# Casting GpSimd loads of q and k in a windowed-attention and spectral-mixing kernel

## The chip, the cores and the metric

The kernel runs on one core of a Trainium2 chip. The core has a matrix engine (PE, with its weight loads shown apart as PEld), a vector engine (DVE), an activation engine (ACT), GpSimd (POOL), a queue engine that only issues transfers (SP), and 16 DMA engines that serve all queues. The metric is the device time of one execution in microseconds. Before the change it is 444.54 us, the median of three runs (444.14 to 446.43).

## The reference, cut to what matters

Attention with a window of 128 positions and a linear distance bias runs over batch 8, 8 heads, 576 positions and 64 features. Its output is mixed over positions in the spectrum: the first 64 modes are each multiplied by a complex 512 x 512 matrix of their own, and the result goes back through the inverse transform. All tensors are float32 in memory.

```python
scores = scale * q @ k.T + slope[h] * -(i - j)       # kept where 0 <= i - j < 128
x = softmax(scores) @ v                              # (8, 576, 512) over all heads
X = rfft(x, axis=1)[:, :64]
Yr = einsum(Xr, w_r) - einsum(Xi, w_i)               # w_r, w_i: (64, 512, 512)
Yi = einsum(Xr, w_i) + einsum(Xi, w_r)
u = x + irfft(Yr + 1j * Yi, n=576)
out = u + relu(u @ w_ch)
```

The 128 matrices of w_r and w_i are 1 MB each and 127 of them are read; q, k and v are 9.4 MB each.

## The kernel before, in words

**Attention.** One unit is a batch and four of its heads: 16 units. For each unit the kernel loads q, k and v, casts them to bf16 on DVE (`cast`), transposes q and k on PE in nine blocks into one PSUM tile (`transpose`, L250), copies that to SBUF as `qkT` (`evacuate`, mostly on ACT, L256), forms the scores (`score`, L271 and L284), applies exp on ACT (`exp`, L294), the mask on DVE (`mask`, L305), multiplies by v (`value`, L331) and divides by the sums on DVE (`norm`, L346 and L347). After the second unit of a batch, `spectrum` and `channels` turn the batch's output into its first 64 modes, `XC`.

**The order of work.** Each engine executes its instructions in the order in which they are written here. `STAGE` lists the steps of one stage with their lags: a step with lag 1 works in stage s on unit s - 1, one with lag -2 on unit s + 2. A stage takes steps of several units, so that all engines have work. There are some preparatory steps before stage 0, written out in the main function.

**The loads.** `load` issues the transfers of q, k and v on SP. The fp32 buffers `raw` hold two units of each. A load of unit u + 2 is issued at the end of the cast of unit u, in whose buffer it lands. One q or k load is 576 KB: 128 partitions, two rows of 2304 bytes each. A v load is five transfers in rows of 512 bytes.

**Early weights.** While attention runs, weights are already read as bf16 by casting loads that POOL issues (`load_w`, L459), into 14 buffers of the pool `early` (one before the stages, one at the end of each of stages 1 to 13) and then into seven stretches of `raw` that are no longer needed (`LATER`, two after stage 13, two after stage 14, three after stage 15). The weight of a stage stands behind a one-element copy on POOL, the gate (L533), which waits for that stage's first `norm`.

**After attention.** The weights go through PE in the order of the modes (L838), four products each. SP loads them plain into a pool of 6 buffers (`NWA`, fp32 read as bf16 by taking every second half-word), later 2 more (`NWB`); eight of the early buffers are used a second time by casting loads on POOL (`AGAIN`). Beside this the finished modes are transposed, and products with w_ch and inverse transforms are made. After the last weight the remaining modes are added and the output is written.

**POOL at the start.** In its order: the identity, the integer tables, the distance tables (`distances`, L147 to L168), the constant parts of the v buffers (`fixtures`, L136 to L140, for two buffers), the first early weight between the two, the end of the Fourier table (L102 to L104), and a memset of `XC` (L496).

Of the kernel before, what the change touches and what calls it, by code (L numbers as in the profile page):

```python
# [10 lines left out]
FP32 = mybir.dt.float32  # L11
BF16 = mybir.dt.bfloat16
# [21 lines left out]

NC = 24


STAGE = (
    ("exp", 1, 0), ("score", 0, 0), ("exp", 0, 0), ("value", 0, 1), ("spectrum", None, 2),
    ("cast", "v", 0), ("score", 2, 0), ("channels", None, 2), ("transpose", "k", -1),  # L40
    ("cast", "k", -2), ("exp", 2, 0), ("norm", 0, 1), ("cast", "q", -3), ("score", 3, 0),
    ("mask", 1, 0), ("value", 1, 1), ("evacuate", "k", -1), ("mask", 0, 0), ("exp", 3, 0),
    ("transpose", "q", -2), ("evacuate", "q", -2), ("score", 1, -1), ("norm", 1, 1),
)
# [62 lines left out]
class _Attention:  # L107


    def __init__(self, tc, ctx, q, k, v, consts, x, XC, raw):  # L110
        self.tc, self.nc = tc, tc.nc
        self.q, self.k, self.v = q, k, v
        self.ident, self.F, self.FT = consts
        self.x, self.XC = x, XC
        B, H, S, _ = q.shape
        self.S, self.NG = S, H // 4
        self.units = [(b, g) for b in range(B) for g in range(self.NG)]
        self.raw = raw
        self.mid = ctx.enter_context(tc.tile_pool(name="amid", bufs=2))
        self.ps = ctx.enter_context(tc.tile_pool(name="aps", bufs=1, space=PSUM))  # L120
        fix = ctx.enter_context(tc.tile_pool(name="afix", bufs=1))
        self.table = fix.tile([P, H, 2, 2 * P], BF16, name="mask")
        self.bias = fix.tile([P, H, 2, 2 * P], BF16, name="bias")
        self.vb = [fix.tile([P, 2, 4, 2, 2 * W], BF16, name=f"vb{i}") for i in range(2)]
        self.vt = [fix.tile([P, 4, 2, W], BF16, name=f"vt{i}") for i in range(2)]
        self.qkT = [fix.tile([P, 2, 2, (FULL + 1) * P], BF16, name=f"qkT{i}") for i in range(2)]
        self.att = [fix.tile([P, FULL * 8 * P + 64], BF16, name=f"att{i}") for i in range(2)]
        self.loaded, self.casted, self.open = {}, {}, {}

    def fixtures(self, i):  # L130
        nc = self.nc
# [66 lines left out]
    def load(self, w, u):  # L198
        nc = self.nc
        if u >= len(self.units):  # L200
            return
        b, g = self.units[u]
        hs = slice(4 * g, 4 * g + 4)
        if w == "v":
            t = self.raw[w][:, u % 2]
            sv = self.v[b, hs]
            for h in range(4):
                nc.sync.dma_start(
                    out=t[:, :2, h],
                    in_=sv[h, : FULL * P].rearrange("(r p j) d -> p r (j d)", r=2, j=2),  # L210
                )
            nc.sync.dma_start(
                out=t[64:96, 2],
                in_=sv[:, FULL * P :].rearrange("h (p j) d -> p h (j d)", j=2),
            )
        else:
            t = self.raw[w][:, u % 2]
            src = (self.q, self.k)["qk".index(w)][b, hs]
            nc.sync.dma_start(
                out=t.rearrange("p e j d -> p e (j d)"),  # L220
                in_=src.rearrange("(e h) (p j) d -> (h p) e (j d)", h=2, j=TPP),
            )
        self.loaded[w, u] = t

    def cast(self, u, w):

        nc = self.nc
        src = self.loaded.pop((w, u))
        if w == "v":
            src = src.rearrange("p s h (j d) -> p s h j d", j=2)  # L230
            for half in range(2):
                row = slice(64 * half, 64 * half + 64)
                nc.vector.tensor_copy(  # L233
                    self.vb[u % 2][row, :, :, :, W * half : W * half + D], src[row, :2])
            nc.vector.tensor_copy(self.vt[u % 2][64:96, :, :, :D], src[64:96, 2])
        else:
            dst = self.mid.tile([P, TPP, 2, D], BF16, tag=w, name=w)
            nc.vector.tensor_copy(dst.rearrange("p j e d -> p e j d"), src)
            self.casted[u, w] = dst
        self.load(w, u + 2)  # L240

    def transpose(self, u, w):
        nc = self.nc
        src = self.casted.pop((u, w))
        if (u, w) == (0, "k"):
            tp = self.ps.tile([P, TPP, P], BF16, tag="sc", bufs=2, name="tp")
        else:
            tp = self.ps.tile([P, TPP, P], BF16, tag="tp", name="tp")
        for j in range(TPP):
            nc.tensor.transpose(tp[:, j], src[:, j].rearrange("p e d -> p (e d)"), self.ident)  # L250
        self.open[w, u] = tp

    def evacuate(self, u, w):
        tp = self.open.pop((w, u))
# [145 lines left out]
def kernel(  # L400
# [11 lines left out]
    ctx.enter_context(tc.manual_schedule(engines=ALL | {SP}))  # L412
    B, H, S, _ = q.shape
    NM, DM, _ = moe_w_r.shape
    AHEAD = {stage: 1 for stage in range(1, 14)}
    LATER = {13: 2, 14: 2, 15: 3}
    EARLY, NWA, NWB, AGAIN = 14, 6, 2, 8
    HM = NM // 2

    const = ctx.enter_context(tc.tile_pool(name="const", bufs=1))  # L420
# [10 lines left out]
        tc.tile_pool(name="w1", bufs=EARLY, side="right", reuse_waits="tile")  # L431
    )
    rawpool = actx1.enter_context(tc.tile_pool(name="raw", bufs=1, side="right"))
    raw = {w: rawpool.tile([P, 2, 2, TPP, D], FP32, name=w + "r") for w in "qk"}
    raw["v"] = rawpool.tile([P, 2, 3, 4, 2 * D], FP32, name="vr")
    spare = [raw[w][:, i].rearrange("p e j d -> p (e j d)") for w in "qk" for i in range(2)]
    vflat = raw["v"].rearrange("p u s h d -> p (u s h d)")
    spare += [vflat[:, 2 * DM * i :] for i in range(3)]
    spare = [t[:, : 2 * DM].bitcast(BF16).rearrange("p (a e) -> p a e", a=4) for t in spare]
    LAST = NM // 4 - 1  # L440
    turns = []
    for g in range(NM // 4):
# [25 lines left out]
    with ExitStack() as actx:  # L468
        at = _Attention(tc, actx, q, k, v, (ident, F, FT), x, XC, raw)
        n = len(at.units)  # L470
        for w, u in (("q", 0), ("k", 0), ("q", 1), ("k", 1), ("v", 0), ("v", 1)):
            at.load(w, u)
        done = set()

        def run(name, arg, u):
            if 0 <= u < n and (name, arg, u) not in done:
                done.add((name, arg, u))
                getattr(at, name)(u, arg)

        make_identity(nc, ident)  # L480
        pool = _Scratch(x[:, B - 2 :].rearrange("p b t c -> p (b t c)").bitcast(FP32))
        wt = at.ps.tile([P, P], FP32, tag="av", bufs=1, name="warm")
        for _ in range(24):
            nc.tensor.matmul(wt, lhsT=ident, rhs=ident, start=True, stop=True)
        table = _forward_table(nc, pool, F, S)
        next(table)
        nc.vector.memset(norm, 2.0 / S)
        nc.vector.memset(norm[:32], 1.0 / S)
        for t in at.qkT:
            nc.vector.memset(t[:, 1, :, S:], 0.0)  # L490
        at.distances(pool)
        at.fixtures(0)
        load_w(1, early, True)
        next(table, None)
        at.fixtures(1)
        nc.gpsimd.memset(XC[:, 4 * NC * NM :], 0.0)  # L496
        run("cast", "q", 0)
        run("transpose", "q", 0)
        run("cast", "k", 0)
        run("transpose", "k", 0)  # L500
        run("evacuate", "q", 0)
        for h in (1, 3):
            at.decay(h)
        run("evacuate", "k", 0)
        run("score", 1, 0)
        for h in (0, 2, 1, 3):
            at.offset(h)
        run("cast", "q", 1)
        run("transpose", "q", 1)
        run("evacuate", "q", 1)  # L510
        run("score", 0, 0)
        run("exp", 1, 0)
        for h in (0, 2):
            at.decay(h)
        run("exp", 0, 0)
        run("cast", "k", 1)
        run("cast", "v", 0)
        side = {0: [(at.offset, 4), (at.offset, 6), (at.decay, 5), (at.offset, 5), (at.decay, 7),
                    (at.offset, 7), (at.decay, 4), (at.decay, 6)]}
        lags = [lag for _, _, lag in STAGE]  # L520
        for stage in range(min(lags), n + max(lags)):
            for name, arg, lag in STAGE:
                run(name, arg, stage - lag)
                if name in ("transpose", "exp") and side.get(stage):
                    for _ in range(1 + (name == "transpose")):
                        fn, h = side[stage].pop(0)
                        fn(h)
            if stage == 3:
                at.inverse_table()
            if stage in AHEAD:  # L530
                if stage:
                    b, g = at.units[stage - 1]
                    nc.gpsimd.tensor_copy(gate[:1, :1], x[:1, b, 0, 256 * g : 256 * g + 1])  # L533
                load_w(AHEAD[stage], early, True)
            if stage in LATER:
                load_w(LATER[stage], None, True)

# [441 lines left out]
```

## Time and profile before

| | |
|---|---|
| median of three runs | 444.54 us |
| span of the profiled execution, which is its time here | 441.7 us |
| PE, PEld busy | 332.8, 179.9 us |
| DVE, ACT, POOL busy | 184.5, 162.1, 50.2 us |
| bytes written by the DMA engines | 156.92 MB |
| bytes read from memory | 162.53 MB |
| q casts, k casts on DVE | 12.7, 12.4 us |
| transposes of q and k on PE | 11.6, 12.2 us |

The profile shows one execution. Its slices cut the span into 40 equal parts and give the busy share of each engine in tenths. Windows give busy time, granted clock, DMA share and GB/s of a stretch; the DMA share counts the time of all packets, and where packets of two queues overlap on an engine it passes 1. GB/s counts bytes as they are written. A timeline line gives start, duration, engine, source line, operation and, in brackets, the idle time before it with what ended it. Issues of transfers on SP and POOL appear as DMA_DIRECT2D.

### The profile page before, as it was taken

Reading aid. Unit: us, or ns where it says so; the run is one execution under the profiler, and the core shown is the slowest. Engines: PE = TensorE matmul, PEld = TensorE weight load, DVE = VectorE, ACT = ScalarE, POOL = GpSimd, SP = SyncE. Lnnn points to the kernel's source line nnn. Section 1 sums busy time; section 2 is a strip of 40 time slices with the busy share of each in tenths; the row PEclk is TensorE's granted clock in tenths of the full one; section 3 lists DMA queues with packets and bytes.
Section 4 is the critical chain, followed back from the end, with each engine's and each line's share of the span. In section 5 each row is a group of like instructions: output and inputs, shape, how many; then the busy total and the mean of one; then the engine's idle time right before and its main releaser. Section 6 shows DMA issues by size and latency. Waiting matters only on the chain. (4 is left out here: it accounts for less than half of the span.)

```text
span 441.7 us, 8410 instructions
## 1 busy us (share of the span) xinstructions
PE 332.8 (75%) x3509; PEld 179.9 (41%) x3509; DVE 184.5 (42%) x332; ACT 162.1 (37%) x211; POOL 50.2 (11%) x107
## 2 busy tenths in 40 slices
PE   5589899879886454454545597999979999879982
PEld 4367677667664221121112133444434444333440
DVE  7789899887863200010000021332222223122694
ACT  6849899978960000000000011232222322101781
POOL 8711010101302200110000000000000000002500
PEclk9969999999998855555555569999999999999998
DMA  8999999999999999999999999999999999997498
GB/s 282 321 325 280 299 322 298 317 294 301 225 214 315 319 316 316 331 383 426 419 422 421 422 422 418 420 421 418 421 419 421 421 418 419 421 422 313 170 376 322
DMA packets 53209, 156.92 MB, mean 355 GB/s; under 512 B 4772, under 2 KB 23860, under 8 KB 40756
## 3 DMA queue, kind: packets, MB, share of 16 engines
q1 hardware_dynamic: 47860, 140.56, 82.2%
q0 software_dynamic: 5312, 15.84, 18.1%
q8 instruction: 27, 0.44, 0.4%
q14 instruction: 10, 0.08, 0.0%
HBM read 162.53 MB, written 9.44 MB: 389 GB/s over the span
## 5 line engine op out<-in xcount | busy, mean ns | idle before, releaser
L838 PE MATMUL acc<-w,XC 128*32 128x512 bf16 x456 | 93.1, 498 | 62.3 <-DMA w<-in_moe_w_r_dram 34.0
L838 PEld LDWEIGHTS <-XC 128*32 128x32 bf16 x508 | 39.4, 149 | 114.5 <-issue 100.1
L294 ACT ACTIVATE att<-sc 128x1024 bf16<-128x1024 f32 x64 | 64.1, 1032 | 10.7 <-PE sc L284 10.6
L604 ACT CAST ZW<-zw 128x512 bf16<-128x512 f32 x8 | 4.7, 585 | 147.6 <-PE zw L602 147.6
L331 PE MATMUL av<-vb,att 128*128 128x132 bf16 (+1 forms) x576 | 38.6, 218 | 10.9 <-DVE x L347 5.9
L331 PEld LDWEIGHTS <-att 128*128 128x128 bf16 x704 | 36.7, 99 | 16.3 <-DVE x L347 10.2
L576 DVE TENSOR_SCALAR yq<-acc 128x512 bf16<-128x512 f32 x14 | 9.6, 686 | 79.6 <-PE acc L838 79.6
L670 PE MATMUL my<-wch,xT 128*64 128x512 bf16 x288 | 34.5, 381 | 5.8 <-ACT x L701 4.3
L679 ACT CAST XW<-my 128x512 bf16<-128x512 f32 x36 | 19.3, 589 | 51.0 <-PE my L627 51.0
L651 DVE COPY xT<-tr 128x1024 bf16<-128x1024 bf16 x18 | 12.4, 691 | 55.0 <-PE tr L649 55.0
L256 ACT COPY qkT<-tp 128x1152 bf16<-128x1152 bf16 x30 | 33.5, 1116 | 2.8 <-PE tp L250 2.1
L616 POOL DMA_DIRECT2D Z<-yq x11 | 5.5, 511 | 217.4 <-issue 216.2
L347 DVE TENSOR_TENSOR x<-av,rec 128x640 bf16<-128x640 f32 x32 | 26.4, 824 | 1.1
L284 PE MATMUL sc<-qkT 64*64 64x256 bf16 (+2 forms) x640 | 25.1, 263 | 2.1 <-ACT qkT L256 1.2
L670 PEld LDWEIGHTS <-xT 128*64 128x64 bf16 x288 | 17.2, 109 | 21.7 <-issue 9.3
L794 DVE TENSOR_TENSOR o<-yy,r 128x1024 f32<-128x1024 f32 (+1 forms) x22 | 21.5, 1024 | 4.3 <-ACT r L770 3.2
L233 DVE CAST vb<-vr 64x1024 bf16<-64x1024 f32 x32 | 22.6, 708 | 0.2
L701 ACT CAST x<-my 128x512 bf16<-128x512 f32 x18 | 10.5, 585 | 33.0 <-PE my L627 33.0
L284 PEld LDWEIGHTS <-qkT 64*64 64x64 bf16 x640 | 14.5, 109 | 19.4 <-issue 16.3
L702 DVE CAST x<-my 128x512 bf16<-128x512 f32 x18 | 12.4, 691 | 23.4 <-PE my L627 23.4
L271 PE MATMUL sc<-bias,ident 128*128 128x512 bf16 x64 | 20.8, 409 | 1.3 <-ACT att L294 1.3
L305 DVE TENSOR_TENSOR att<-att,mask 128x1024 bf16<-128x1024 bf16 x32 | 20.6, 683 | 0.0
(130 smaller groups left out, 396.6 us busy)
## 6 DMA issues: line engine op xcount, KB each, us to landing
w<-in_moe_w_i_dram SPq DMA_DIRECT2D x49, 1024.0 KB, 17.9
w<-in_moe_w_r_dram SPq DMA_DIRECT2D x48, 1024.0 KB, 16.0
qr<-in_q_dram SPq DMA_DIRECT2D x16, 576.0 KB, 10.3
kr<-in_k_dram SPq DMA_DIRECT2D x16, 576.0 KB, 8.6
vr<-in_v_dram SPq DMA_DIRECT2D x64, 128.0 KB, 7.6
out_dram<-o SPq DMA_DIRECT2D x13, 512.0 KB, 4.5
w<-in_moe_w_r_dram POOLq DMA_DIRECT2D x12, 512.0 KB, 8.8
w<-in_moe_w_i_dram POOLq DMA_DIRECT2D x10, 512.0 KB, 8.3
```

The lines of the kernel that those rows point to most:

```text
L233: nc.vector.tensor_copy(self.vb[u % 2][row, :, :, :, W * half : W * half + D], src[row, :2])
L256: (self.nc.vector.tensor_copy if u < 2 and w == "q" else self.nc.scalar.copy)(dst.rearrange("q h (p j) -> q h p j", j=TPP), tp.rearrange(" ...
L271: nc.tensor.matmul(sc[:, e], lhsT=self.ident, rhs=self.bias[:, hv].rearrange("p j n -> p (j n)"), start=True, stop=False, skip_group_check ...
L284: nc.tensor.matmul(sc[64 * half : 64 * half + 64, e, j * 256 + c0 : j * 256 + c0 + n], lhsT=qkT[row, 1, h, k0 + j : k0 + P : 2], rhs=qkT[r ...
L294: self.nc.scalar.activation(self.att[u % 2][:, kt * 8 * P : (kt + 1) * 8 * P], sc.rearrange("p e n -> p (e n)"), AF.Exp, scale=1.0 / math. ...
L305: nc.vector.tensor_tensor(out=rows, in0=rows, in1=self.table[:, heads], op=ALU.mult)
L331: nc.tensor.matmul(bank[:, qt * W : qt * W + rhs[j].shape[1]], lhsT=att[:, o : o + P], rhs=rhs[j], start=(n == 0 and j == 0), stop=(n == l ...
L347: nc.vector.tensor_tensor(out=self.x[:, b, :, cs].rearrange("p t (h d) -> p h t d", h=2), in0=tiles[:, :, :, :D], in1=rec.unsqueeze(-1).br ...
L670: nc.tensor.matmul(mm[ROWS[half]], lhsT=lhsT, rhs=wch[:, dt], start=(dt == 0), stop=False, skip_group_check=True,)
L679: nc.scalar.copy(XW[:, j, n], mms[n])
L794: nc.vector.tensor_tensor(out=o[:, c], in0=yy[:, c], in1=r[:, c], op=ALU.add)
L838: nc.tensor.matmul(into[32 * (m % 4) : 32 * (m % 4) + 32], lhsT=XC[:, c0 : c0 + 31 * NM + 1 : NM], rhs=wq[t][a], start=(ri == 0 and a == 0 ...
```

## The change

q and k are loaded by POOL instead of SP, as transfers that cast float32 to bfloat16. Their buffers are bf16, three units deep, and PE transposes them directly: each block as two groups of 64 columns, one for each pair of heads. The DVE casts of q and k are gone, and the load of unit u + 3 is issued after the transposes of unit u. The three pairs of loads of the start are set between POOL's preparatory work. The smaller buffers leave room for 17 early weights; `AHEAD` loads two at stages 5, 8 and 11, and six stretches of `raw` are used late. The pool of plain weights has 5 buffers and then 3 more.

```diff
-    ("cast", "k", -2), ("exp", 2, 0), ("norm", 0, 1), ("cast", "q", -3), ("score", 3, 0),
+    ("exp", 2, 0), ("norm", 0, 1), ("score", 3, 0),
...
-            t = self.raw[w][:, u % 2]
+            t = self.raw["qk"][:, u % NQK, "qk".index(w)]
             src = (self.q, self.k)["qk".index(w)][b, hs]
-            nc.sync.dma_start(
+            nc.gpsimd.dma_start(
...
     def transpose(self, u, w):
         nc = self.nc
-        src = self.casted.pop((u, w))
+        src = self.loaded.pop((w, u))
...
         for j in range(TPP):
-            nc.tensor.transpose(tp[:, j], src[:, j].rearrange("p e d -> p (e d)"), self.ident)
+            for e in range(2):
+                nc.tensor.transpose(tp[D * e : D * e + D, j], src[:, e, j], self.ident)
         self.open[w, u] = tp
+        self.load(w, u + NQK)
...
-    AHEAD = {stage: 1 for stage in range(1, 14)}
-    LATER = {13: 2, 14: 2, 15: 3}
-    EARLY, NWA, NWB, AGAIN = 14, 6, 2, 8
+    AHEAD = {stage: 1 + (stage in (5, 8, 11)) for stage in range(1, 14)}
+    LATER = {12: 1, 13: 1, 14: 2, 15: 2}
+    EARLY, NWA, NWB, AGAIN = 17, 5, 3, 8
...
-    raw = {w: rawpool.tile([P, 2, 2, TPP, D], FP32, name=w + "r") for w in "qk"}
-    raw["v"] = rawpool.tile([P, 2, 3, 4, 2 * D], FP32, name="vr")
...
+    raw = {"qk": rawpool.tile([P, NQK, 2, 2, TPP, D], BF16, name="qkr"),
+           "v": rawpool.tile([P, 2, 3, 4, 2 * D], FP32, name="vr")}
...
-        for w, u in (("q", 0), ("k", 0), ("q", 1), ("k", 1), ("v", 0), ("v", 1)):
+        for w, u in (("q", 0), ("k", 0), ("v", 0), ("v", 1)):
             at.load(w, u)
...
         next(table)
+        at.load("q", 1)
+        at.load("k", 1)
...
         at.distances(pool)
+        at.load("q", 2)
+        at.load("k", 2)
         at.fixtures(0)
         load_w(1, early, True)
         next(table, None)
         at.fixtures(1)
         nc.gpsimd.memset(XC[:, 4 * NC * NM :], 0.0)
-        run("cast", "q", 0)
         run("transpose", "q", 0)
-        run("cast", "k", 0)
         run("transpose", "k", 0)
...
-        run("cast", "q", 1)
         run("transpose", "q", 1)
...
-        run("cast", "k", 1)
         run("cast", "v", 0)
```

More of the change, by code (lines that the diff above doesn't have):

```diff
@@ L35 @@
 NC = 24
+NQK = 3
 STAGE = (
@@ L127, in __init__ @@
         self.att = [fix.tile([P, FULL * 8 * P + 64], BF16, name=f"att{i}") for i in range(2)]
-        self.loaded, self.casted, self.open = {}, {}, {}
+        self.loaded, self.open = {}, {}
     def fixtures(self, i):
@@ L204, in load @@
         if w == "v":
-            t = self.raw[w][:, u % 2]
+            t = self.raw["v"][:, u % 2]
             sv = self.v[b, hs]
@@ L216, in load @@
         else:
-            t = self.raw[w][:, u % 2]
+            t = self.raw["qk"][:, u % NQK, "qk".index(w)]
             src = (self.q, self.k)["qk".index(w)][b, hs]
-            nc.sync.dma_start(
+            nc.gpsimd.dma_start(
                 out=t.rearrange("p e j d -> p e (j d)"),
@@ L227, in cast @@
         nc = self.nc
[L228 to L239, printed above, removed]
+        src = self.loaded.pop((w, u)).rearrange("p s h (j d) -> p s h j d", j=2)
+        for half in range(2):
+            row = slice(64 * half, 64 * half + 64)
+            nc.vector.tensor_copy(
+                self.vb[u % 2][row, :, :, :, W * half : W * half + D], src[row, :2])
+        nc.vector.tensor_copy(self.vt[u % 2][64:96, :, :, :D], src[64:96, 2])
         self.load(w, u + 2)
@@ L433 @@
     rawpool = actx1.enter_context(tc.tile_pool(name="raw", bufs=1, side="right"))
-    raw = {w: rawpool.tile([P, 2, 2, TPP, D], FP32, name=w + "r") for w in "qk"}
-    raw["v"] = rawpool.tile([P, 2, 3, 4, 2 * D], FP32, name="vr")
-    spare = [raw[w][:, i].rearrange("p e j d -> p (e j d)") for w in "qk" for i in range(2)]
+    raw = {"qk": rawpool.tile([P, NQK, 2, 2, TPP, D], BF16, name="qkr"),
+           "v": rawpool.tile([P, 2, 3, 4, 2 * D], FP32, name="vr")}
+    spare = [raw["qk"][:, u % NQK].rearrange("p w e j d -> p (w e j d)")[:, : 4 * DM]
+             for u in range(B * H // 4 - NQK, B * H // 4)]
     vflat = raw["v"].rearrange("p u s h d -> p (u s h d)")
-    spare += [vflat[:, 2 * DM * i :] for i in range(3)]
-    spare = [t[:, : 2 * DM].bitcast(BF16).rearrange("p (a e) -> p a e", a=4) for t in spare]
+    spare += [vflat[:, 2 * DM * i : 2 * DM * (i + 1)].bitcast(BF16) for i in range(3)]
+    spare = [t.rearrange("p (a e) -> p a e", a=4) for t in spare]
     LAST = NM // 4 - 1
```

## The prediction

> **What bounds the kernel now.** I read the page's slices first, then its queue table, then the windows view over stretches in which one kind of transfer runs nearly alone, then the timelines of POOL and of the attention stages.
>
> ```profile
> PE   5589899879886454454545597999979999879982
> DVE  7789899887863200010000021332222223122694
> DMA  8999999999999999999999999999999999997498
> GB/s 282 321 325 280 299 322 298 317 294 301 225 214 315 319 316 316 331 383 426 419 422 421 422 422 418 420 421 418 421 419 421 421 418 419 421 422 313 170 376 322
> ...
> q1 hardware_dynamic: 47860, 140.56, 82.2%
> q0 software_dynamic: 5312, 15.84, 18.1%
> ```
>
> The 16 DMA engines are taken from the first slice to the 36th. GB/s counts bytes written, so a casting load (fp32 read, bf16 written) shows at half of what it reads; the dip in slices 11 and 12 is that, not a pause. The two queues together make 100.3% of the span.
>
> ```profile
> 20.00:22.00 2.00, 0.00 (x0) 0.00 (x0) 0.51 (x2) 1.90 (x3) 0.00 (x0) 1.00 1.05 383
> 30.00:31.00 1.00, 1.00 (x23) 1.00 (x21) 0.15 (x1) 0.73 (x1) 0.00 (x0) 1.00 1.15 270
> 33.00:121.00 88.00, 78.90 (x1439) 60.88 (x1436) 75.88 (x137) 78.25 (x88) 13.37 (x29) 0.98 1.07 292
> 37.00:40.00 3.00, 2.76 (x61) 2.39 (x58) 2.92 (x7) 2.93 (x4) 0.00 (x0) 1.00 0.98 209
> 116.00:120.00 4.00, 3.89 (x76) 3.03 (x73) 2.79 (x6) 3.70 (x5) 2.90 (x6) 1.00 0.95 193
> 121.00:133.00 12.00, 10.31 (x195) 7.93 (x194) 7.96 (x14) 8.15 (x10) 1.29 (x3) 1.00 1.06 217
> 200.00:395.00 195.00, 152.26 (x1051) 64.76 (x1050) 39.85 (x77) 32.20 (x58) 0.00 (x0) 0.84 1.01 421
> ```
>
> Columns: stretch, length, busy of PE, PEld, DVE, ACT, POOL, granted clock, DMA share, GB/s. q and k loads nearly alone move 383 GB/s (first row), v loads 270 (second), casting weight loads 217 written, so 434 read (sixth), plain weight loads 421 (last). In the steady attention (third row) the DMA share is 1.07, full for two queues side by side. The gates on POOL stand at 27.38 and 115.80 and twelve stages lie between them: 7.37 us each. One stage asks the DMA engines for q and k, 1.18 MB at 383 (3.1 us), v, 0.59 MB at 270 (2.2 us), and one weight, 1.05 MB at 434 (2.4 us): 7.7 us, a little over the stage itself, as the kinds overlap slightly. ACT works 78.25/88 of a stage, 6.6 us, PE the same, DVE 6.4. So the DMA engines bound attention too, closely followed by the rest, and from the first packet at 3.2 us to the last weight near 406 us they lose under 1 us: the rows at 37 and 116 lack (1.07 - 0.98) x 3 and (1.07 - 0.95) x 4, some 0.7 us. The end is then 406 us plus a tail of 35 us that the change does not touch. What counts is the work given to the DMA engines and the time in which they have none.
>
> **The change part by part.** The profiled execution spans 441.7 us; the median of the runs is 444.54, so 2.8 us lie around the span, and I add them at the end.
>
> *DVE casts.* 16 of q at 795 ns and 16 of k at 774 ns go: 25.1 us, 1.6 us a stage. Their cover is the DMA time of the same stage, so I count 0. If that cover were gone, a stage could fall from 7.37 us to the 6.6 of ACT, 0.8 us each.
>
> *The same bytes as casting loads.* q and k are still read as 18.9 MB of fp32, in rows of 2304 bytes. A casting load of 8192-byte rows ran at 434 GB/s read where the plain one ran at 421, 3% better; in the trace's packet records a casting packet of the 1 KB bf16 rows of wch took 90 ns on average and a plain 2 KB output packet 88, 2% worse. On the 49 us that q and k occupy (18.9/0.383) that is -1.5 to +1.0 us. I take 0.
>
> *More early weights.* 17 + 6 instead of 14 + 7 move two megabytes of reading from after attention to before it; the sum of DMA work is unchanged: 0. The pool of plain weights shrinks from 6 to 5 buffers until the first recycled ones are used up; with two in use and three in flight (7.5 us at 421 GB/s) I take 0, at worst 2 us.
>
> *Transposes.* Now 18 of 64 columns instead of 9 of 128. Nine cost 0.66 to 0.68 us at full clock. If the two column halves run side by side, as the 64-column products of L670 do (288 in 34.5 us, 120 ns each for 512 columns), nothing is added; if each half costs as much as a whole one, 0.68 us more, 1.4 us a stage. PE at 6.6 us a stage has 0.8 us to spare before it passes the DMA time. I take 0; the far end is 0.6 us over, 16 times: 10 us.
>
> *POOL's queue.* This is the part that decides.
>
> ```profile
> 7.46 0.97 POOL L136 MEMSET vb<- 64x1056 bf16 x1
> ...
> 11.36 0.75 POOL L459 DMA_DIRECT2D w<-in_moe_w_r_dram  x1
> ...
> 18.28 0.96 POOL L496 MEMSET XC<- 128x1024 bf16 x1
> 27.38 0.64 POOL L533 COPY gate<-x 1x1 bf16<-1x1 bf16 x1 [8.14 <-DVE x L347]
> 27.96 0.55 POOL L459 DMA_DIRECT2D w<-in_moe_w_r_dram  x1
> ...
> 10.91 0.37 SPq L219 DMA_DIRECT2D qr<-in_q_dram  x1
> 11.50 0.37 SPq L219 DMA_DIRECT2D kr<-in_k_dram  x1
> ```
>
> Now SP issues the third q and k loads at 10.91 and 11.50 us, and POOL works without a pause on tables, fixtures and the XC memset until 19.24. After the change six q/k loads are issued between these POOL pieces, and the loads of unit 3, though their buffers are free early (they wait only for the transposes of unit 0), stand behind the XC memset. An issue on POOL costs 0.53 us (the usual one) to 0.76 us (the first one; wch), six of them 3.2 to 4.6, taken as 3.6: the load of q of unit 3 is issued at 22.8 us (22.4 to 23.8). From issue to first packet the weights issued on POOL up to 116 us, when nothing of their queue is ahead of them, needed 2.65 to 5.6 us, median 3.8 (packet records; 11.36 to 16.95 is the longest, SP's first load needed 2.4). So its data begin at 26.6 us (25.1 to 29.4). What the DMA engines have until then: six q/k loads, 3.54 MB at 383 (9.2 us); v of units 0, 1, 2, 1.77 MB at 270 (6.6 us; v of unit 3 waits for the second v cast, now at 23.8); one weight (2.4 us). That is 18.2 us of work from 3.2 us on, done at 21.4 if it is all there in time. They idle 26.6 - 21.4 = 5.2 us (3.7 to 8.0). Nothing gives this back: the work is the same and the engines were full everywhere else. Compute is hardly hurt: the third unit's q and k are loaded by then. The POOL pieces ahead of the first scores slip by the four issues before them, about 2.4 us, partly paid by the two casts that fall away; that is hidden as well.
>
> The Trainium skill, DMA: Bandwidth & Descriptors, section Specifications, puts the first byte of a GpSimd load at about 1 us. By that rule the idle time would be 22.8 + 1.0 - 21.4 = 2.4 us in place of 5.2. The Trainium skill, SBUF — State Buffer, section SBUF: two separate sides, speaks against the change: while DVE runs a copy in a two-port mode, GpSimd can't write descriptors. The packet records, with 2.65 to 5.6 us, side with the second page, and I go by them.
>
> *Later in attention.* In stage order POOL now issues k, then q (after the transposes near the end of a stage), then gate and weight, so weights start a few us later in a stage. The loads lead by three units instead of two, so no wait appears. v stays on SP alone and shares the engines with one full queue instead of half of one; when v is late DVE's queue stops at its cast, with norms and masks behind it, and the releases stop with it; meanwhile the engines still have v to move. From stage 12 on eight weights are left to cover the end of attention instead of nine, 2.4 us less, from which a backlog must come. I set this against the 0.7 us of idle time that may go: 0 (-0.7 to +2).
>
> Sum: 441.7 + 5.2 = 446.9 us of span, with 2.8 around it 449.7.
>
> **The rivals.**
>
> *Startup gap hidden (no change).* If descriptors are written faster with DVE idle than in the rows above (near the 2.1 us in which the small Z loads land altogether) and memsets run shorter without DVE casts beside them, q of unit 3 begins at 23.5 and the gap is 2.1 us, less 0.7: 446 us. Against it: the 5.6 us row is from just this phase.
>
> *Cheaper q and k loads (faster).* q and k move 383 GB/s in rows of 2304 bytes where 8192-byte rows move 421: 9% go to the packets. If the GpSimd queue doesn't pay that, 49 us become 44.6, and DVE and ACT have the room to follow, since 7.37 us a stage would fall by 0.3. With the gap hidden as above that is 444.5 + 2.1 - 0.7 - 4.4 = 441.5 us; with the gap of 5.2 us it takes a saving of over 5.2/49, 11%, before the sign turns. For it: casting weights are 3% faster than plain ones. Against it: wch's 2 KB packets, nearest in size, are not.
>
> *PE takes over (slower still).* The 18 transposes don't pair, PE reaches 8.0 us a stage, and the DMA engines run dry between gates: 449.7 + 10 = 460 us. Against it: L670's pairs.
>
> *The engines run dry late.* With v starved beside the full GpSimd queue or the cover at the end missing, 449.7 + 3 = 453 us.
>
> **How the numbers follow.** Forecast (gap of 3.7 to 8 us, rest hidden): 0.58. Late dryness: 0.10. PE: 0.08. Gap hidden: 0.16. Cheaper loads: 0.08. The measurement can tell about 0.5%, 2.2 us, from no change; slower by more is 0.58 + 0.10 + 0.08, less a little for the forecast's low end: 0.74; same 0.18; faster 0.08. The range runs from 444.0 (half of the hidden case and the faster one left out) to 457 (PE's far end left out).
>
> **What would show it.** Right: a DMA slice of 6 to 8 tenths near 20 to 27 us; the XC memset ending near 23; the last weight landing near 411; DVE near 159 us; stages of 7 to 7.5 us. Wrong: the DMA share at 1 or more from 15 to 30 us; attention stages well under 7 us with the first plain weight before 130 us; or L250 near 1.3 us for a set of transposes and gates 8 us apart.

## The result and the profile after

The changed kernel takes 449.15 us (median of seven runs, 446.56 to 454.1); the kernel before takes 444.54 (443.96 to 446.43). The ratio is 1.0084, with a 95% interval of 1.0056 to 1.0113: 3.7 us slower (2.5 to 5.0). Ratios here compare only runs within 1.5% of the fastest of their kernel, so the run of 454.1 us counts in the medians, which lie 4.6 us apart, and not in the 3.7. The execution in the profile is one of the longer ones: it took 451.47 us with a span of 449.4, where the span before was 441.7.

These are the slices and queues of the page after, the same rows as shown of before (busy tenths in 40 slices of 11.2 us, then packets, MB and share of the 16 DMA engines).

```profile
PE   4778969699398653454455477999998999789882
DVE  4846465565367320000101012322312232112594
DMA  9999999999998999999999999999999999998498
GB/s 174 205 198 219 227 230 221 223 219 223 217 194 166 318 320 318 316 337 384 424 421 421 421 421 419 418 421 421 419 421 421 419 419 419 422 419 327 164 378 312
...
DMA packets 53212, 146.48 MB, mean 326 GB/s; under 512 B 4772, under 2 KB 32052, under 8 KB 41012
...
q1 hardware_dynamic: 38868, 119.59, 68.6%
q0 software_dynamic: 14304, 26.32, 31.8%
```

GB/s is lower through attention because bf16 is written where fp32 was (146.48 MB in place of 156.92); the bytes read are the same. PE and DVE both stand at 3 tenths in the eleventh slice (112 to 124 us), and the dip to 166 GB/s comes one slice later than before. The DMA row says 9 nearly everywhere and is no help: where two queues overlap, the share of a full slice is 1.1 to 1.2, so one of 0.95 is a loss and still prints as 9. The windows show it. First before, then after (stretch, length, busy PE, PEld, DVE, ACT, POOL, granted clock, DMA share, GB/s):

```profile
17.00:26.00 9.00, 3.48 (x46) 2.98 (x47) 7.44 (x13) 4.90 (x7) 2.12 (x4) 0.80 1.07 329
108.00:120.00 12.00, 11.08 (x208) 8.81 (x204) 10.28 (x19) 11.03 (x13) 3.93 (x8) 1.00 1.02 246
120.00:150.00 30.00, 23.39 (x346) 16.06 (x344) 15.29 (x35) 9.70 (x13) 6.26 (x12) 0.94 1.05 274
```

```profile
17.00:26.00 9.00, 5.98 (x119) 4.44 (x119) 6.93 (x12) 8.29 (x10) 8.78 (x14) 1.00 0.97 203
26.00:108.00 82.00, 68.07 (x1351) 53.28 (x1362) 48.65 (x90) 63.48 (x71) 24.36 (x43) 0.94 1.13 222
108.00:120.00 12.00, 5.68 (x126) 4.14 (x124) 3.29 (x6) 7.04 (x8) 1.38 (x3) 0.87 1.09 220
120.00:150.00 30.00, 24.67 (x441) 19.92 (x444) 20.77 (x39) 17.35 (x20) 5.13 (x10) 0.88 0.94 187
```

Against 1.13 in the stretch from 26 to 108 us, the rows at 17 (0.97) and at 120 (0.94) lack work. Two places, then. The first is POOL's queue at the start, in POOL's timeline after:

```profile
1.27 0.91 POOL L221 DMA_DIRECT2D qkr<-in_q_dram  x1 [0.82 <-POOLq L962]
...
9.79 0.74 POOL L221 DMA_DIRECT2D qkr<-in_q_dram  x1
10.52 0.72 POOL L221 DMA_DIRECT2D qkr<-in_k_dram  x1
...
20.72 1.09 POOL L499 MEMSET XC<- 128x1024 bf16 x1
21.77 0.70 POOL L221 DMA_DIRECT2D qkr<-in_q_dram  x1
22.46 0.71 POOL L221 DMA_DIRECT2D qkr<-in_k_dram  x1
```

The loads of unit 3 stand behind the XC memset, as forecast, and are issued at 21.77 us; the packet records, counted from the start of the span as the windows count them, have their first packet at 23.23. The same queue opens an earlier, smaller hole. The six q and k loads of the start thin out from 15.5 us on, v of unit 2 is issued at 15.37 behind the first v cast and has its first packet at 17.8, and the first weight, which POOL issues at 14.84 where it did at 11.36 before, has its first packet at 16.28. The windows, first before, then after:

```profile
15.00:17.00 2.00, 1.55 (x22) 0.96 (x19) 1.98 (x3) 2.00 (x4) 1.94 (x3) 1.00 1.10 315
```

```profile
15.20:16.80 1.60, 0.85 (x17) 0.48 (x15) 1.57 (x6) 1.60 (x3) 1.44 (x6) 1.00 0.82 101
```

The second place is a stage of 13.8 us late in attention. DVE's and POOL's timelines and the waits up to 150 us (engine, line, waited for: total, times, longest) show it:

```profile
109.25 0.82 DVE L345 TENSOR_TENSOR x<-av,rec 128x640 bf16<-128x640 f32 x1
118.16 1.39 DVE L233 CAST vb<-vr 64x1024 bf16<-64x1024 f32 x2 [8.08 <-DMA vr<-in_v_dram]
```

```profile
107.89 0.42 POOL L532 COPY gate<-x 1x1 bf16<-1x1 bf16 x1
108.27 1.11 POOL L458 DMA_DIRECT2D w<-in_moe_w_i_dram  x2
121.69 0.51 POOL L532 COPY gate<-x 1x1 bf16<-1x1 bf16 x1 [12.31 <-DVE x L345]
```

```profile
DVE vb L233 <- DMA vr<-in_v_dram: 23.5, 7, 8.1
...
POOL gate L532 <- DVE x L345: 18.0, 2, 12.3
```

DVE waits 8.1 us for v with the norms queued behind its cast, POOL's gate waits for those norms, and POOL can issue no further weight. Before, DVE's 32 casts of v had 0.2 us of idle time ahead of them in all. In the packet records of 114.8 to 118.8 us, 46.5 packets of casting weights (8 KB read each) and 50.5 packets of v (512 bytes each) move per us, about one for one, while v nearly alone moves some 600 a us: so v crawls beside a full GpSimd queue.

To put one measure on these places I worked out from the packet records of each run how much DMA time its packets need, each kind at the time that one packet took an engine when its kind ran nearly alone (casting weights 305 ns, plain weights 311, q and k 94 before and 89.4 as casting loads, v 26.6), divided by 16 engines, and took it from the length of each stretch, from the first packet (1.8 us) to the last weight. What is left is time lost, in us. Semaphore writes and instruction fetches are not counted as work; they make some 5 us of what is lost in each run, so it is differences between rows that count.

| | last weight lands | work | lost in all | to 17 | 17–26 | 26–108 | 108–160 |
|---|---|---|---|---|---|---|---|
| before | 406.4 | 396.3 | 8.2 | 1.2 | 0.4 | 2.7 | 2.4 |
| after | 414.0 | 394.0 | 18.2 | 2.6 | 2.0 | 4.2 | 7.5 |

The last weight lands 7.6 us later, and the span is 7.7 longer: the tail did not change. The work fell by 2.3 (the casting q and k packets are 5% shorter) and the loss rose by 10.0: 3.0 at the start (1.4 before 17 us, 1.6 after it), 5.1 at the end of attention, 1.5 between, 0.4 elsewhere. This execution is 2.3 us above the median one, so the late place is probably larger here than usually.

### The profile page after: what moved, and what is told of

Same layout as the page of the kernel before. It is cut to its first block, busy times and chain, and to the rows that moved or that the text cites. A ratio compares the mean times of both kernels' runs of the same rounds, so it can differ in the third digit from the quotient of the medians.

```text
span 449.4 us, 8928 instructions
## 1 busy us (share of the span) xinstructions
PE 329.7 (73%) x3776; PEld 182.6 (41%) x3797; DVE 161.9 (36%) x300; ACT 161.4 (36%) x211; POOL 71.5 (16%) x141
## 2 busy tenths in 40 slices
DMA packets 53212, 146.48 MB, mean 326 GB/s; under 512 B 4772, under 2 KB 32052, under 8 KB 41012
## 5 line engine op out<-in xcount | busy, mean ns | idle before, releaser
L837 PE MATMUL acc<-w,XC 128*32 128x512 bf16 x460 | 88.7, 475 | 60.9 <-DMA w<-in_moe_w_r_dram 32.3
L329 PE MATMUL av<-vb,att 128*128 128x132 bf16 (+1 forms) x576 | 41.1, 226 | 15.7 <-DVE x L345 15.6
L329 PEld LDWEIGHTS <-att 128*128 128x128 bf16 x704 | 39.5, 103 | 21.4 <-DVE x L345 17.9
L233 DVE CAST vb<-vr 64x1024 bf16<-64x1024 f32 x32 | 22.3, 696 | 23.7 <-DMA vr<-in_v_dram 23.5
L282 PE MATMUL sc<-qkT 64*64 64x256 bf16 (+2 forms) x640 | 26.1, 271 | 4.5 <-ACT qkT L254 1.4
L247 PE MATMUL tp<-ident,qkr 128*64 128x128 bf16 x576 | 24.1, 233 | 6.4 <-DMA qkr<-in_q_dram 3.0
L669 PEld LDWEIGHTS <-xT 128*64 128x64 bf16 x288 | 17.1, 109 | 21.8 <-issue 9.3
L247 PEld LDWEIGHTS <-qkr 128*64 128x64 bf16 x576 | 19.4, 117 | 9.4 <-DMA qkr<-in_q_dram 3.4
```

Of the source, the lines that this page charges most:

```text
L233: nc.vector.tensor_copy(self.vb[u % 2][row, :, :, :, W * half : W * half + D], src[row, :2])
L247: nc.tensor.transpose(tp[D * e : D * e + D, j], src[:, e, j], self.ident)
L282: nc.tensor.matmul(sc[64 * half : 64 * half + 64, e, j * 256 + c0 : j * 256 + c0 + n], lhsT=qkT[row, 1, h, k0 + j : k0 + P : 2], rhs=qkT[r ...
L329: nc.tensor.matmul(bank[:, qt * W : qt * W + rhs[j].shape[1]], lhsT=att[:, o : o + P], rhs=rhs[j], start=(n == 0 and j == 0), stop=(n == l ...
L669: nc.tensor.matmul(mm[ROWS[half]], lhsT=lhsT, rhs=wch[:, dt], start=(dt == 0), stop=False, skip_group_check=True,)
L837: nc.tensor.matmul(into[32 * (m % 4) : 32 * (m % 4) + 32], lhsT=XC[:, c0 : c0 + 31 * NM + 1 : NM], rhs=wq[t][a], start=(ri == 0 and a == 0 ...
```

## The experiments

Theory A: the time is lost at the start, because POOL issues the loads of unit 3 too late. Theory B: it is lost later, because v alone on SP is starved beside a GpSimd queue that is now always full. Rivals: the 64-column transposes, the extra early weights, or DVE. All ratios are against the kernel before, run beside them, with 95% intervals.

**Unit 3 loaded before the second fixtures and the XC memset (A undone).**

```diff
         load_w(1, early, True)
+        run("transpose", "q", 0)
+        run("transpose", "k", 0)
         next(table, None)
         at.fixtures(1)
         nc.gpsimd.memset(XC[:, 4 * NC * NM :], 0.0)
-        run("transpose", "q", 0)
-        run("transpose", "k", 0)
```

> The changed kernel with the transposes of unit 0 written ahead of the second fixtures, so that POOL issues the loads of unit 3 at about 15.6 us and not at 21.8; nothing else moves. Theory A (the prediction's): the loss is the gap at the start; the DMA share in 17 to 26 us goes back to 1.05 or more and 3 to 5 us of the 4.6 come back, 444.5 to 446 us. Theory B (v, alone on SP's queue beside a full GpSimd queue, comes late, attention stretches and the engines lack work at its end): the gap closes, but the time falls by 2 us at most, 447 us or more, and DVE still waits over 15 us for v.

Measured: 445.42 us, ratio 0.9998 (0.9979 to 1.0017): all of the loss is gone. Its windows and its longest wait for v:

```profile
17.00:26.00 9.00, 6.63 (x141) 5.06 (x146) 6.95 (x13) 8.55 (x10) 8.28 (x14) 1.00 1.15 231
...
120.00:150.00 30.00, 24.83 (x434) 18.99 (x438) 17.97 (x34) 17.13 (x22) 5.28 (x11) 0.94 1.04 252
```

```profile
DVE vb L233 <- DMA vr<-in_v_dram: 25.4, 10, 5.3
```

The loads of unit 3 are issued at 15.03 us and the share at 17 to 26 us is 1.15 in place of 0.97. DVE still waits 25.4 us for v, as B says, and the kernel is level with the one before all the same. That does not make those waits free: the cheaper q and k packets pay for part of the loss, and with v moved as well ("both edits" below) another 1.2% comes off. What is gone beside the gap is the long stage at the end of attention (share 1.04 in place of 0.94 from 120 us on), which the edit does not touch.

**v on POOL's queue from unit 4 on (B undone).** v goes through the same queue as q, k and the weights, in order of need, as three transfers instead of five.

```diff
             sv = self.v[b, hs]
+            if u >= 4:
+                for r in range(2):
+                    nc.gpsimd.dma_start(
+                        out=t[:, r],
+                        in_=sv[:, 2 * P * r : 2 * P * (r + 1)].rearrange(
+                            "h (p j) d -> p h (j d)", j=2),
+                    )
+                nc.gpsimd.dma_start(
+                    out=t[64:96, 2],
+                    in_=sv[:, FULL * P :].rearrange("h (p j) d -> p h (j d)", j=2),
+                )
+                self.loaded[w, u] = t
+                return
```

> The changed kernel with v from unit 4 on issued by POOL too, three transfers a unit, so that q, k, v and weights stand in one queue in the order in which they are needed. The start is untouched. Theory B: DVE's wait for v (23.5 us) falls under 8 us, no stage is longer than 9 us, the engines are full from 110 to 140 us, and 3 to 5 us come back: 444 to 446 us. Theory A: v was late only because the engines were behind from the start; waits move from v to q and k, and the time stays within 1 us of 449.

Measured: 441.84 us, 0.9926 (0.9904 to 0.9948): faster than the kernel before, with the gap of the start still there.

```profile
17.00:26.00 9.00, 6.61 (x139) 5.00 (x138) 7.94 (x14) 8.41 (x10) 8.08 (x14) 1.00 0.89 179
...
120.00:150.00 30.00, 21.84 (x357) 16.36 (x357) 16.46 (x36) 9.74 (x13) 7.64 (x15) 1.00 1.05 274
```

The share is 0.89 at the start and 1.05 from 120 us on. By the measure above, the loss from 26 to 108 us falls from 4.2 to 1.1 us and that from 108 to 160 from 7.5 to 0.8, and the work from 394.0 to 392.2, since the GpSimd queue moves eight 512-byte rows of v as one packet (last section). The gain, 7 us on the changed kernel, is more than the 3 to 5 expected, although DVE still waits 14.4 us for v and not under 8. So v on its own queue cost more than its longest wait shows.

**Both edits.** The two diffs above together.

> The changed kernel with both edits: the transposes of unit 0 ahead of the second fixtures, and v from unit 4 on issued by POOL. If the gap at the start (theory A) and v's queue (theory B) are two separate costs, the gains add: the first took 0.9% off the changed kernel, the second 1.6%, together a ratio to before of 0.98 to 0.987, 436.5 to 439.5 us. If they are two ways to the same idle time at the end of attention, the ratio stays at 0.99 or more, 440.5 us and up.

Measured: 440.26 us, 0.9874 (0.9854 to 0.9894).

```profile
17.00:26.00 9.00, 6.33 (x132) 4.80 (x133) 6.99 (x13) 8.86 (x11) 8.19 (x14) 1.00 1.15 234
...
120.00:150.00 30.00, 21.29 (x319) 16.92 (x310) 16.17 (x36) 7.33 (x11) 7.46 (x15) 0.89 1.03 279
```

With v in POOL's queue, closing the gap is worth 0.9926 - 0.9874 = 0.52%, or 2.3 us (the two intervals leave 0.1 to 0.9%). With the gap closed, moving v is worth 0.9998 - 0.9874 = 1.24%, 5.5 us. The gains of the two edits alone, 0.86 and 1.58%, add up to 2.44%; together they give 2.10%. So they are for the most part two separate costs.

**The extra weights at stages 11, 12 and 13.** If B's long stage comes from running out of cover, more weights late should help.

```diff
-    AHEAD = {stage: 1 + (stage in (5, 8, 11)) for stage in range(1, 14)}
+    AHEAD = {stage: 1 + (stage in (11, 12, 13)) for stage in range(1, 14)}
```

> The changed kernel with the second weight of stages 5 and 8 moved to stages 12 and 13: as many early weights, two more of them for the end of attention. Theory B: v is held up less in stages 5 to 9 and the end has 4.9 us more to move; the share from 130 to 150 us goes to 1.0 or more and 2 to 4 us come back: 445 to 447 us. Theory A: the same work at another time, within 1 us of 449.

Measured: 452.95 us, 1.0138 (1.0098 to 1.0177), a miss. The additional weights are issued in the same stages as the last v loads, and one v is held up longer: from DVE's timeline,

```profile
125.37 1.39 DVE L233 CAST vb<-vr 64x1024 bf16<-64x1024 f32 x2 [11.38 <-DMA vr<-in_v_dram]
```

the wait is 11.4 us in place of 8.1, and the gates on POOL stand 17.0 us apart there. More weights late do not shorten the long stage, which speaks against lack of cover and for v behind weights. It is not a proof: the interval overlaps the changed kernel's, and the profiled execution loses 5.3 us from 26 to 108 us and 5.8 from 108 to 160, in sum about what the changed kernel loses.

**Three v buffers.** v gets a lead of three units; to make room, early weights go from 17 to 15 and the late stretches from six to seven.

```diff
-            t = self.raw["v"][:, u % 2]
+            t = self.raw["v"][:, u % 3]
...
-        self.load(w, u + 2)
+        self.load(w, u + 3)
...
-    AHEAD = {stage: 1 + (stage in (5, 8, 11)) for stage in range(1, 14)}
-    LATER = {12: 1, 13: 1, 14: 2, 15: 2}
-    EARLY, NWA, NWB, AGAIN = 17, 5, 3, 8
+    AHEAD = {stage: 1 + (stage in (8,)) for stage in range(1, 14)}
+    LATER = {12: 1, 13: 1, 14: 2, 15: 3}
+    EARLY, NWA, NWB, AGAIN = 15, 5, 3, 8
```

> The changed kernel with three buffers of v instead of two (load of unit u + 3 after the cast of u, units 0 to 2 at the start), on SP as before; for the room 15 early weights instead of 17 and seven late stretches instead of six. v's packets and queue stay, only its lead grows by a stage. Theory B: DVE's wait for v falls from 23.5 us to under 8 us, no stage is longer than 10 us, and 2 to 5 us come back, 444 to 447 us. If v's lateness is a symptom of engines that are full, the wait goes to q and k and the time stays at 448 us or more.

Measured: 448.01 us, 1.0042 (1.0019 to 1.0066). DVE's waits for v fall from 23.5 to 15.0 us, the longest from 8.1 to 5.7; a stage of 11.1 us is left though no weights are doubled near it. By the point estimates half of the loss comes back; the intervals overlap.

**14 early weights, one a stage.**

```diff
-    AHEAD = {stage: 1 + (stage in (5, 8, 11)) for stage in range(1, 14)}
+    AHEAD = {stage: 1 for stage in range(1, 14)}
...
-    EARLY, NWA, NWB, AGAIN = 17, 5, 3, 8
+    EARLY, NWA, NWB, AGAIN = 14, 5, 3, 8
```

> The changed kernel with 14 early weights instead of 17, one a stage; all else as it is, six late stretches and 5 + 3 plain buffers included. The prediction counted the number of early weights as 0, since the same bytes move sooner or later: 448 to 451 us. If the weights beside v are what makes v late, DVE's wait for v falls under 15 us and the time to 447 us or less; if the engines lack them as cover, it rises to 452 us or more.

Measured: 448.58 us, 1.007 (1.0044 to 1.0096), not to be told from the changed kernel: the number of early weights is worth nothing that these runs can tell. Its profile has the gap (2.5 us lost from 17 to 26 us) and no long stage at the end (2.3 us lost from 108 to 160).

**Before, with transposes of 64 columns.** This part of the change alone.

```diff
-            nc.tensor.transpose(tp[:, j], src[:, j].rearrange("p e d -> p (e d)"), self.ident)
+            for e in range(2):
+                nc.tensor.transpose(tp[D * e : D * e + D, j], src[:, j, e], self.ident)
```

> The kernel before with one part of the change alone: each transpose as two groups of 64 columns. The prediction counted 0, with 0.68 us a set at the far end. If the halves pair, a set of 18 takes 0.66 to 0.75 us and the time is that of before within 0.5 us (444 to 445); if they don't, a set takes 1.3 us and PE's 1.4 us a stage show as 3 us or more, 447 us and up.

Measured: 445.95 us, 1.0009 (0.9988 to 1.003). A set in PE's timeline of this kernel:

```profile
106.68 0.69 PE L251 MATMUL tp<-ident,k 128*64 128x128 bf16 x18
```

Eighteen transposes of 64 columns take 0.69 us, and in the trace of before nine of 128 take 0.66 to 0.68: the halves run side by side.

**DVE's casts given back.** Before each set of transposes DVE makes two casts whose output nobody reads. They take 513 ns each, together 1.03 us where the removed cast took 0.77 to 0.80: in all units, then from unit 4 on only, and then these on top of "both edits".

```diff
         src = self.loaded.pop((w, u))
+        for e in range(2):                      # second kernel: range(2 if u >= 4 else 0)
+            idle = self.mid.tile([P, TPP, D], FP32, tag="idle", bufs=1, name="idle")
+            nc.vector.tensor_copy(idle, src[:, e])
```

> The changed kernel with DVE's load given back: ahead of each set of transposes two casts of the bf16 q or k into an unused fp32 buffer, nothing else. The prediction counted 0 for the casts that went, since the DMA engines cover them. If so, the time stays within 1% of the changed kernel, 446 to 453 us. If DVE's freed time is worth its 1.6 us a stage, 12 to 25 us are lost: 460 us and up.

> The changed kernel with the two unused DVE casts ahead of each set of transposes from unit 4 on only, so that the start is untouched. Giving DVE its load back in all units cost 0.8%. If that came at the start, where POOL's memsets and descriptors share time with DVE, this one stays at the changed kernel's time, ratio to before 1.006 to 1.011, 448 to 450 us. If it came in the steady stages, where v is late and DVE's queue stands behind it, the 0.8% show again: ratio 1.013 or more, 451 us and up.

> The kernel with both edits (unit 3 early, v on POOL), which keeps the DMA engines full, with the same unused DVE casts from unit 4 on. If the DMA engines cover DVE's work as the prediction had it, its ratio of 0.987 stays within 0.003, 438 to 441 us. If DVE's time lies on the path, or keeps POOL from writing descriptors, the ratio rises to 0.993 or more, 442 us and up.

Measured: 454.15 us, 1.0168 (1.0138 to 1.0197), in all units; 447.88 us, 1.0061 (1.0031 to 1.0091), from unit 4 on; 439.31 us, 0.9857 (0.9831 to 0.9882), on top of both edits. From unit 4 on the casts cost nothing that can be told in either kernel: DVE's relief in the steady stages is worth 0 within some 0.3%. The same casts in the first four units as well cost 1.0168 - 1.0061, some 1%. Why was not found; DVE is then also busy with the tables, and everything there is ahead of the first releases. The second kernel's windows:

```profile
17.00:26.00 9.00, 7.06 (x154) 5.15 (x146) 7.94 (x14) 8.34 (x10) 8.01 (x14) 1.00 0.90 182
...
120.00:150.00 30.00, 23.06 (x423) 18.38 (x426) 20.89 (x42) 17.31 (x22) 4.22 (x9) 1.00 1.05 232
```

Here the gap is there (0.90) and the long stage at the end is not (1.05). A stage of 13.3 us stands earlier, from 50.7 us on, but the loss from 26 to 108 us is as in the first experiment: a long stage alone need not cost anything. Against that experiment, which has neither gap nor late long stage, this is 1.0061 - 0.9998 = 0.63%, 2.8 us (the two intervals leave 0.1 to 1.1%): a second price of the gap beside the 2.3 us from both edits.

**Before, with v on POOL from unit 4 on.** The edit of the second experiment on the old kernel, to see whether its gain is in v's packets alone.

> The kernel before with v from unit 4 on issued by POOL, three transfers a unit; q and k stay on SP with their DVE casts. It tells apart why v on POOL helped the changed kernel. If a transfer of 512-byte rows is cheaper on the GpSimd queue (its packets there are recorded with 4096 bytes and not 512), before gains too, 3 to 5 us: 440 to 442 us. If only the order of the queue mattered, before, where v and q and k shared SP's queue, gains nothing: 444 us or more.

Measured: 448.27 us, 1.0056 (1.0039 to 1.0074): a loss.

```profile
108.00:120.00 12.00, 8.67 (x134) 7.37 (x134) 8.19 (x16) 7.31 (x9) 4.50 (x8) 0.86 0.84 223
120.00:150.00 30.00, 24.10 (x390) 17.63 (x389) 16.14 (x34) 13.56 (x17) 9.37 (x17) 0.94 0.95 236
```

The engines run short at the end of attention, where v now stands behind the gates on POOL (0.84 and 0.95, where before had 1.02 and 1.05). The rows of v are merged here too, and it did not decide. The experiment moved two things at once, so it gives no price of the packets.

**Both edits and three v buffers.** With the settings of the three-buffer experiment on top of "both edits".

> Both edits, and three buffers of v with 15 early weights and seven late stretches. DVE still waits 13 us for v with both edits. If the engines are full there, a longer lead gives nothing: ratio 0.985 to 0.990, 438.5 to 441 us. If the waits cost time at the end of attention, 1 to 2 us more come back: ratio 0.983 or less.

Measured: 438.26 us, 0.9841 (0.9813 to 0.9868), the shortest of all, though its interval overlaps that of both edits. From 120 us on its window is

```profile
120.00:150.00 30.00, 18.92 (x265) 13.44 (x262) 10.55 (x26) 4.02 (x7) 6.49 (x12) 0.93 1.05 284
```

with attention nearly over (ACT 4.0 us of 30, 17.4 after the change): the stages end earlier and the engines stay full. The loss measure for the kernels that separate the causes:

| | last weight lands | work | lost in all | to 17 | 17–26 | 26–108 | 108–160 |
|---|---|---|---|---|---|---|---|
| unit 3 early | 407.4 | 394.0 | 11.6 | 2.3 | 0.7 | 4.4 | 2.5 |
| casts back from unit 4 | 409.8 | 394.0 | 14.0 | 2.2 | 2.5 | 4.5 | 3.4 |
| 14 early weights | 409.3 | 394.1 | 13.4 | 2.3 | 2.5 | 4.7 | 2.3 |
| v on POOL | 404.2 | 392.2 | 10.1 | 2.2 | 2.6 | 1.1 | 0.8 |
| both edits | 402.5 | 392.6 | 8.0 | 2.1 | 0.6 | 1.7 | 1.2 |
| both, three v buffers | 400.7 | 392.2 | 6.6 | 1.7 | 0.2 | 0.9 | 0.7 |

(The merged v packets, at 192 ns, are told from weight packets by their duration, so "work" is good to some 0.5 us in the last three rows.) The hole before 17 us is in all the changed kernels and least with three v buffers, whose v of unit 2 is asked for at once.

## Why the prediction was right, and where its sizes were not

The time (449.7 forecast, 449.15 measured), its sign and the bound were right: what the DMA engines are asked for, and the time in which they have nothing, set the end. The sum agrees with the median better than its terms deserve: it added 5.2 us, the ratio of the runs says 3.7 (2.5 to 5.0), and three terms were off in ways that offset each other. Of the 2.8 us that it put around the span only some 2.0 lies there (451.47 against 449.4 in the execution profiled after); the rest is that the profiled execution before was a short one.

**The clock of the packet records.** The prediction counted packets from about 1.3 us before the start of the span. It has the first packet at 3.2 us, but the row

```profile
0.00:3.00 3.00, 1.64 (x16) 1.65 (x17) 1.01 (x3) 1.28 (x1) 2.06 (x14) 1.00 0.34 111
```

of the kernel before shows a third of a megabyte moved by 3.0 us, and DVE casts the first k at 5.91, which by that count would be ahead of its last packets. On the clock of the span the first packet comes at 1.85 us, the weights of before needed 1.3 to 4.25 us from issue to first packet, median 2.5, and SP's first load 1.1. The forecast of 5.2 us is hardly touched: both the end of the work (20.0 in place of 21.4) and the first packet of unit 3 (25.3 in place of 26.6) move with the clock.

**POOL's queue, counted at 5.2 us (3.7 to 8.0): the right mechanism, mis-sized.** By the loss measure the start cost 3.0 us, and 3.1 to 3.2 in the kernels with the gap alone, below the stated low end. Two steps made it too large. The load of q of unit 3 was issued at 21.8 us, not 22.8: POOL's preparatory pieces ran shorter, although the six issues took 4.6 us (0.72 to 0.91 each) where 3.6 were counted. Its first packet came 1.5 us after the issue, the near end of the 1.3 to 4.25 us and not the median. That makes 1.0 + 1.0 us, and 5.2 becomes 3.2. One more step failed without changing the sum: the work was not "all there in time". It ran short once near 16 us (1.4 us more lost than before) and again from 21.5 us until the data of unit 3 came (1.6); what the second hole held was v of unit 3, issued at 20.6 us because the second v cast stood at 18.8 and not 23.8. Issuing unit 3 early closes only the second hole, worth 2.3 us (v on POOL, with and without the early loads) and 2.8 (casts back against unit 3 early), with intervals that reach 4 and 5 us.

The Trainium skill, DMA: Bandwidth & Descriptors, section Specifications, puts the first byte of a GpSimd load at about 1 us. The deciding load needed 1.5 us from issue to first packet, nearer to that than to the median of 2.5, so the packet records did not speak against this page as the prediction had it. The other page weighed, SBUF — State Buffer, section SBUF: two separate sides, on DVE holding up GpSimd's descriptors, was not settled: DVE copies beside POOL's issues cost nothing that can be told from unit 4 on and 1% before it, and no run shows whether descriptor writing had a part in that.

**Later in attention, counted at 0 (-0.7 to +2).** The rival "engines run dry late" was priced at 3 us, with v starved beside the full GpSimd queue as one of its two causes. That is what the profiled execution shows: 5.1 us more lost from 108 to 160 us and 1.5 between 26 and 108. (The prediction's "under 1 us" of idle time in the kernel before was low as well: the measure leaves some 3 us there beside semaphore writes and fetches.) The late part is not in every execution. The kernels with the gap and no late long stage stand at 1.0061 and 1.007, the changed kernel at 1.0084, intervals overlapping; its own runs spread from 446.56 to 454.1. That the upper ones hold the long stage and the lower ones do not is argued from this, not shown, since only one was profiled. The step that failed is "meanwhile the engines still have v to move": v moves one small packet for each weight packet, and POOL's gate behind DVE's norm stops the weights once the wait is long. The part between 26 and 108 us stays without the long stage too (4.4 to 4.7 us lost in "unit 3 early" and the two kernels with the gap alone, against 2.7 before) and goes with v on POOL (1.1 to 1.7). In the changed kernel POOL's issues of q and k also wait 50.3 us in all for transposes, with gates and weights behind them; how much of that part this makes, no run separates.

**The same bytes as casting loads, counted at 0 (-1.5 to +1.0).** By the rate of q and k nearly alone, a row of 2304 bytes takes 89.4 ns of an engine where it took 94: 8192 packets over 16 engines, 2.4 us less, a little beyond the bound. This is the rival "cheaper q and k loads", at 5% in place of its 9%. It offsets much of the loss: with the gap closed and no late long stage the kernel stands at 0.9998, the cheaper packets against the additional loss before 17 us and between 26 and 108. No run has these loads alone.

**DVE casts, transposes, early weights: 0 each.** All three held within what the runs can tell: 1.0061 with DVE's work from unit 4 on and 1.0084 without it, 1.0009 for the transposes, 1.007 with 14 early weights. Outside the text's view was that casts in the first units are not free.

**What would show it.** DVE at 161.9 us (159 forecast), the XC memset ending at 21.8 (23) and transposes far from 1.3 us a set are as stated. The last weight in the profiled execution lands 7.6 us later, not 5; in the two kernels with the gap alone 3 us later. The stages take 7.8 us on average up to the gate at 107.89 and then 13.8, not 7 to 7.5. The slice of 6 to 8 tenths near 20 to 27 us did not appear, for the reason given with the slices: the sign to name was the share of a window against its neighbours.

**Open.** Why closing the gap at the start also removes the long stage at the end; what makes the loss between 26 and 108 us besides v; the price of v's cheaper packets apart from their place in the queue; and what in the first units makes DVE's work cost time.

## What to carry to other kernels

Where transfers are the bound, moving a load to another engine's queue did not by itself make its transfer dearer here: list what stands ahead of it on the new queue and work out when the DMA engines run out; then check when each piece of that work is asked for, since it need not be there in time, and check that the times you compare stand on one clock. A stream of small rows left alone on a second queue moved here at the pace of the other queue's packets. In the same queue in order of need it gained 1.6% on the changed kernel, but the same move cost the kernel before 0.6%, where v came to stand behind the gates; more lead gave back half of the loss by the point estimates. A wait shown in the profile costs little as long as the engines have other packets, and costs in earnest when what waits also holds back the next issues.

## What the runs showed of the hardware that was not expected

- The GpSimd queue merges rows. With v on it, the page of that kernel has

```profile
DMA packets 40731, 146.47 MB, mean 333 GB/s; under 512 B 4388, under 2 KB 17844, under 8 KB 28532
```

in place of 53212 packets: eight 512-byte rows go as one packet of 4096 bytes, some 192 ns each, where eight single ones on SP's queue take 8 x 26.6 = 213 ns. The casting loads of q and k stay one packet a row.
- Two queues that were both full shared the engines by packets, not by bytes: 46.5 packets of 8 KB to 50.5 of 512 bytes per us.
- The loads of q and k took less time per row as casting loads than as plain ones: 89.4 against 94 ns for 2304 bytes read.
